# Two of four blocks of a four-tap filter, from VectorE products to diagonal matmuls on TensorE

## The chip, the cores and the metric

The kernel runs on one core of a Trainium2 chip. The metric is the device time of one execution in microseconds (us). The profile names the engines PE (TensorE, with its weight loads PEld), DVE (VectorE), ACT (ScalarE), POOL (GpSimd) and SP (SyncE, which here only issues DMAs).

## The reference

Two independent parts share one kernel; their outputs lie side by side, 576 columns each, for 2048 rows.

```python
# A: sliding dilated attention, 32 heads of 18, 8 positions with a distance of 2
qkv = x @ wqkv
logits = einsum("bhsd,bhswd->bhsw", q, kg) * scale      # kg, vg: k, v at s - 2 w
o = einsum("bhsw,bhswd->bhsd", softmax(logits), vg)
a = o @ wo
# B: a long convolution over the sequence, per channel
for t in range(4):                                        # the four taps
    k_shift = k_shift + k_pad[:, t:t + S, :] * shift_k[:, 3 - t]
kv = k_shift * v
y = irfft(rfft(kv, 2 S) * rfft(ssm_k, 2 S))[:S] + kv * ssm_D
b = q * y
```

The change is in the four taps of B, k_shift, for rows 1024 to 2047.

## The kernel before

All data is bf16, all sums are made in PSUM in fp32. Part B cuts the 2048 rows into four blocks of 512. Each block of kv is transformed by matmuls with tables of sines (`x_unit`), so is each block of the filter (`filter_unit`), their products are made by DVE (`spectral_product`), summed by PE (`spectral_sum`), and turned back by PE (`inverse`). Part A projects q, k and v on PE (`project`), multiplies q and k on DVE (`pair_product`, L706), sums over a head on PE (`pair_sum`, L720), takes the softmax, multiplies by v on DVE (`weigh`, L813) and sums on PE (`weighted`, L824; `output`, L888).

There is no scheduler. Every step is a job with a short name, and the string ORDER at the top lists the jobs; they are written out in that order, and each engine does its own instructions in it, one after the other. The names that matter here:

- `Lk2`, `Lv2`, `Lk3`, `Lv3`: loads of blocks 2 and 3 of k and v, on SP (L184, L203). Blocks 0 and 1 are loaded ahead of the written order.
- `T0` to `T3`: the taps of a block (L511). k was loaded as seven shifted rows for each group of four, with the channel along the row, so that a tap is a product with `skb`, the taps spread over all partitions (L517), a sum (L520), and at the end a product with v (L536), all on DVE. The result, kv, lies in `xw` at `kv_of(i)`.
- `M30` and the like: `mirror` (L538), matmuls with the matrix `fold` on PE, which make sums and differences of a row and its mirror row. Rows from both halves of a block lie on even and odd partitions.
- `k00a`, `k00b`, `q13a` and the like: halves of a projection, four matmuls each (L322, 128 x 128 weights, 512 columns); the second half also has the last 64 channels as two matmuls of 64 rows (L333). `X5` transposes the last 64 channels of x.
- `L001`, `G001`: pair product on DVE and pair sum on PE. `K310`: filter unit. `F3`: folding of a filter block (L602), `Lf3` its transposing load (L213), `Lo3` and `Fr` small copies on POOL and SP. `x001`: transform of a block of kv. `Lw`, `RG0`: weights of v and their regrouping. `SV` opens the memory that the taps used for part A's products.
- `I0`, `I1`: tables for the way back (L397): matmuls with 128 x 64 weights and 128 columns, in pairs on the two column halves of the array.

PSUM is four buffers that are handed out in turn (`banks`); a step that asks for one waits until whoever had it has been copied out.

Of the kernel before, what the change touches and what calls it, by code (L numbers as in the profile page):

```python
# [19 lines left out]
ORDER = """  # L20
    T0 k03a' T1 S1 k03b I1 k02a k02b Lk2 Lv2 I0 k00a' Lk3 Lv3 M01 X5 k00b q10a Ex q10b Lf3 T2 Lo3 q13a' q13b
    k10a k10b T3 k13a' Lf2 k13b q12a q12b N2 Lo2 k01a M10 k01b Lf1 M00 k11a k11b q11a M11 q11b Lf0 N3 Lw SV L001
    k12a M20 k12b x001 M21 x021 q24a x020 q24b x000 Lo1 k24a Fr Lo0 Z2 N1 RG3 k24b RG2 F3 RG0 F2 L000 K310 G000
    K311 K210 K211 L002 K313 G001 RG4 F1 G002 L003 G003 K302 L004 G004 K301 L010 K212 L011 K303 K213 K203 N0 F0
    L012 K200 K300 G010 L013 K201 K312 K202 RG1 G011 G012 K113 K103 G013 L014 G014 K112 K102 K101 L100 K100 K010
    K111 K110 sm0a K001 K013 sm0b v24a' L101 v24b L102 G100 L103 G101 K012 sm0c sm0d U3 U2 K000 K011 K003 G102
    K002 D0 D1 v11a v11b G103 L104 G104 ak00 M30 v12a' v12b ak02 v01a ak01 L110 G110 M31 L111 G111 v01b v00a'
    L112 G112 L113 Wl v00b G113 x031 U1 L114 G114 V04 v10a' v10b A04 sm1a sm1b v02a v02b v03a' sm1c v03b x201
    V10 V11 sm1d V12 A10 v13a' v13b D2 x330 x310 x301 V13 A11 V20 V21 x200 x331 x230 x010 x221 A20 x321 V22 x210
    x011 V23 D3 V34 ax02 x220 x030 x300 D4 A21 V40 V41 A34 D5 O000' x211 V42 x320 x231 x111 x131 Tx2 A40 V43  # L30
    x120 x101 ax00 x130 ax01 V50 x121 x311 O001 A41 V51 O100' p000 x100 x110 O010 A50 V52 z000 O011' V53 O101
    A51 Tk2 p010 z010 ax10 O020' O021 p020 z020 O110' ak10 i000 p200 i02880 Q0 p100 z100 p101 p110 p111 Q1 z101
    i02881 i001 p121 p120 O111 z110 p201 z111 z120 p210 z121 O120 p211 z200 z210 z211 p212 z212 z201 p202 z202
    Tx3 p220 Tk3 p221 O030' p222 O121 b0288 z220 p301 z221 O031' p302 b00 z222 p303 i200 i100 g0 Q2 p300 y300
    p312 i12880 i201 i101 i12881 z300 z301 z303 p310 p311 y310 O130 b10 b1288 p313 g1 Q3 p322 O131' z310 p320
    z311 p321 z313 i22880 i300 b20 y320 p323 i22881 i301 b2288 g2 z320 z321 z323 b30 i3384L g30 g3384
"""
# [14 lines left out]
def kernel(  # L52
# [122 lines left out]
    def kTok(m):  # L175
        return view(Ks, k_at(m, 2), [[D, 4], [1, D]])
    kjs, vts = [], []

# [5 lines left out]
    def load_k(i):  # L184

        eng = nc.sync
        kj = sp1.tile([128, 7, D], BF16, name="kj", bufs=2)
# [13 lines left out]
        kjs.append(kj)  # L201

    def load_v(i):  # L203
        vt = sp1.tile([128, 4, D], BF16, name="vt", bufs=2)
        nc.sync.dma_start(vt[0:128:2], vf[BL * i:BL * i + 256, :].rearrange("(p c) d -> p c d", c=4))
        nc.sync.dma_start(vt[1:128:2], bass.AP(tensor=vf.tensor, offset=vf.offset + (BL * i + 256 + 3) * D,
                                              ap=[[4 * D, 64], [-D, 4], [1, D]]))
        vts.append(vt)

# [51 lines left out]
    for h in range(2):  # L261
# [6 lines left out]
    nc.gpsimd.tensor_scalar(flip2[:], flip[:], 2.0, None, op0=ALU.mult)  # L268
# [242 lines left out]
    def taps(i):  # L511
# [24 lines left out]
        tt(kv, kv, vt, ALU.mult)  # L536

    def mirror(i, n):  # L538

        kv = kv_of(i)  # L540
        pss, held = zip(*[banks("ps_fold") for _ in range(2)])
        for pm in range(2):
            for h in range(2):
                for e in range(2):
                    nc.tensor.matmul(pss[pm][64 * e:64 * e + 64, h, 0:HD], fold[:, 64 * pm:64 * pm + 64],  # L545
                                     kv[:, 2 * n + e, HD * h:HD * h + HD], start=True, stop=True, tile_position=(0, 64 * e))
        for pm in range(2):
            nc.scalar.activation(halves(kv[:, 2 * n + pm, :]), pss[pm][:, :, 0:HD], ACT.Copy)
        slots.extend(held)

    for i in range(NBL):
        job(f"T{i}", taps, i)
        for n in range(2):
# [582 lines left out]
```

## Time and profile before

| | |
|---|---|
| time, three runs | 206.07, 206.62, 206.96 us; median 206.62 |
| span of the profiled execution | 204.6 us |
| PE busy | 196.9 us, 2074 matmuls and 2074 weight loads |
| DVE busy | 192.3 us, 146 instructions |
| ACT busy | 155.6 us, 223 instructions |
| POOL busy | 60.8 us, 106 instructions |
| mean granted TensorE clock | 0.994 |

The span is what the profile shows of one execution, from the first to the last instruction. Its own time as a run is not listed apart; the median of the runs is 2.0 us above the span. In a group's row stand the line, the engine, the operation, out<-in, the shape and the count; then busy time and the mean of one in ns; then the idle time of the engine before it and what ended it. Matmuls are pipelined: the mean of one holds its way through the array, so the distance from one start to the next is read from the chain or the timeline. In a row of the chain or the timeline stand the start, the length, the engine, the line and the count. In a row of DMA issues the last number is the median time from issue to landing.

### The profile page before, as it was taken

The numbers are of one execution on the slowest core, as the hardware profiler recorded it, in microseconds if no ns is written. First come the engines' busy times: TensorE is split into PE (matmuls) and PEld (weight loads), VectorE is DVE, ScalarE is ACT, GpSimd is POOL, SyncE is SP. The second block draws the span as 40 slices with busy tenths as digits, with TensorE's granted clock in tenths as the row PEclk, the third lists the DMA queues.
The fourth block names the chain that finished last, engine by engine and source line by source line (L and its number), as shares of the span: only waits on it lengthen the run. The fifth ranks groups of instructions, "written<-read, shape, count | busy, mean of one in ns | idle before, by whom it ended". The sixth has DMA issues, their size and how long they took to land.

```text
span 204.6 us, 5004 instructions
## 1 busy us (share of the span) xinstructions
PE 196.9 (96%) x2074; PEld 109.9 (54%) x2074; DVE 192.3 (94%) x146; ACT 155.6 (76%) x223; POOL 60.8 (30%) x106
## 2 busy tenths in 40 slices
PE   7999999999989999999999999999999999999990
PEld 2543544334455646543245556776666767766660
DVE  7559999999999999999999999999999999899992
ACT  4788995678899999966578678886778767767760
POOL 8989500011348581400380000004090001030300
PEclk9999999999999999999999999999999999999997
DMA  6999899989509869999899990879989303944555
GB/s 197 280 293 306 175 289 373 214 177 281 169 3 146 111 82 185 167 180 222 157 235 216 248 244 34 141 183 334 186 227 233 100 28 122 227 130 145 153 182 150
DMA packets 34916, 38.48 MB, mean 188 GB/s; under 512 B 17523, under 2 KB 28911, under 8 KB 34894
## 3 DMA queue, kind: packets, MB, share of 16 engines
q1 hardware_dynamic: 26668, 24.29, 46.5%
q0 software_dynamic: 5760, 11.36, 29.5%
q10 hardware_dynamic: 2466, 2.51, 3.6%
q8 instruction: 16, 0.26, 0.5%
q14 instruction: 6, 0.05, 0.1%
HBM read 13.11 MB, written 4.72 MB: 87 GB/s over the span
## 4 chain that ended last, share of the span: by engine, by line
PE 88%; DMA 3%; ACT 2%; DVE 2%; issue 1%; SPq 1%; DVEq 0%
PE ps_proj L322 18%; PE ps_fx L682 8%; PE ps_wo L888 8%; PE ps_z L975 8%; PE ps_inv L1010 7%; PE ps_acc L824 7%; PE ps_fk L567 5%; PE ps_log L720 5%; DMA Ks<-in_A_x_dram 3%; PE ps_proj L333 3%; PE ps_proj L326 3%; PE ps_proj L439 3%; PE ps_fk L568 3%; PE ps_fold L545 2%; PE ps_wo L880 1%
## 5 line engine op out<-in xcount | busy, mean ns | idle before, releaser
L322 PE MATMUL ps_proj<-xw 128*128 128x512 bf16 x160 | 38.5, 380 | 0.0
L706 DVE TENSOR_TENSOR av<-qk 128x4096 bf16<-128x4096 bf16 (+1 forms) x16 | 31.7, 2014 | 0.1
L322 PEld LDWEIGHTS <-xw 128*128 128x128 bf16 x160 | 13.9, 98 | 19.4 <-issue 5.7
L988 ACT ACTIVATE av<-ps_z 128x768 bf16<-128x768 f32 x23 | 17.2, 811 | 6.5 <-PE ps_z L975 6.0
L517 DVE TENSOR_TENSOR tB<-kj,skb 128x4608 bf16<-128x4608 bf16 (+1 forms) x8 | 19.3, 2416 | 0.1
L950 DVE TENSOR_TENSOR qk<-xw,Ks 128x2304 bf16<-128x2304 bf16 x14 | 18.9, 1354 | 0.3 <-PE ps_z L975 0.3
L684 ACT ACTIVATE xw<-ps_fx 128x576 bf16<-128x576 f32 x32 | 18.6, 665 | 0.3 <-PE ps_fx L682 0.2
L618 ACT ACTIVATE Ks<-ps_fk 128x576 bf16<-128x576 f32 x32 | 18.6, 699 | 0.2 <-PE ps_fk L568 0.2
L355 ACT ACTIVATE qk<-ps_proj 128x1024 bf16<-128x1024 f32 x14 | 14.3, 1023 | 5.2 <-PE ps_proj L333 2.8
L888 PE MATMUL ps_wo<-qk 128*128 128x288 bf16 x128 | 17.9, 287 | 0.0
L626 POOL DMA_DIRECT2D Ks<-Ks x8 | 10.1, 1426 | 26.0 <-PE ps_back L1059 19.3
L682 PE MATMUL ps_fx<-xw,TB 128*128 128x288 bf16 x128 | 17.7, 287 | 0.0
L567 PE MATMUL ps_fk<-Ks,TB 128*128 128x384 bf16 x62 | 16.5, 327 | 0.1
L824 PE MATMUL ps_acc<-av,ident 64*64 64x512 bf16 x160 | 15.3, 378 | 0.0
L1010 PE MATMUL ps_inv<-av,TI 128*128 128x288 bf16 (+1 forms) x112 | 15.2, 292 | 0.0
L568 PE MATMUL ps_fk<-Ks,TB 128*128 128x192 bf16 x62 | 15.2, 246 | 0.0
L682 PEld LDWEIGHTS <-TB 128*128 128x128 bf16 x128 | 11.9, 98 | 5.9 <-issue 2.7
L888 PEld LDWEIGHTS <-qk 128*128 128x128 bf16 x128 | 11.7, 98 | 5.4 <-issue 2.7
L355 ACT ACTIVATE v<-ps_proj 128x1024 bf16<-128x1024 f32 x9 | 9.3, 1033 | 6.5 <-PE ps_proj L322 4.5
L813 DVE TENSOR_TENSOR av<-Ks,v 128x4096 bf16<-128x4096 bf16 x6 | 13.5, 2286 | 0.0
L827 ACT ACTIVATE qk<-ps_acc 128x1024 bf16<-128x1024 f32 x8 | 8.2, 1024 | 6.7 <-PE ps_acc L824 6.7
L1010 PEld LDWEIGHTS <-TI 128*128 128x128 bf16 x112 | 10.6, 98 | 4.2 <-issue 1.1
(195 smaller groups left out, 441.6 us busy)
## 6 DMA issues: line engine op xcount, KB each, us to landing
Ks<-Ks POOLq DMA_DIRECT2D x8, 576.0 KB, 7.8
TB<-av SPq DMA_DIRECT2D x12, 256.0 KB, 5.4
kj<-in_B_k_dram SPq DMA_DIRECT2D x6, 504.0 KB, 7.0
vt<-in_B_v_dram SPq DMA_DIRECT2D x8, 288.0 KB, 5.3
Ks<-av SPq DMA_DIRECT2D x8, 256.0 KB, 5.6
out_dram<-qk ACTq DMA_DIRECT2D x5, 288.0 KB, 3.7
Ks<-in_A_x_dram SPq DMA_DIRECT2D x2, 576.0 KB, 5.4
xw<-in_A_wqkv_dram SPq DMA_DIRECT2D x2, 576.0 KB, 6.2
```

The costliest lines, as they stand in the source:

```text
L322: nc.tensor.matmul(ps[:, jp, :], wq(kb, comp, 128 * ct, 128), xT(kb, 1024 * jj + 512 * jp, 512), **se)
L355: nc.scalar.activation(view(t, o + pad + 1024 * jj, [[512, 2], [1, 512]]), ps[:], ACT.Copy)
L517: tt(to, view(kj, row * D, [[D, n], [D, 4], [1, D]]), view(skb, row * D, [[D, n], [0, 4], [1, D]]), ALU.mult)
L567: nc.tensor.matmul(o[:, 0:2], w, rhs[:, 0:2], start=start, stop=stop)
L568: nc.tensor.matmul(o[:, 2], w, rhs[:, 2], start=start, stop=stop)
L618: nc.scalar.activation(view(Ks, k_at(m, cs ^ (m & 1)) + 96 * gi, [[768, 3], [384, 2], [1, 96]]), acc3(ps), ACT.Copy, scale=(PSG, MSG)[cs][ ...
L682: nc.tensor.matmul(ps[:, pm, 0:HD], TX[:, 2 * pm + c, 128 * gi:128 * gi + 128], kv[:, 2 * c + pm, HD * h:HD * h + HD], start=(c == 0), sto ...
L706: tt(view(P, at, [[step, 4], [256, nj], [1, 256]]), view(t, o + 256 * hh, [[0, 4], [512, nj], [1, 256]]), view(tk, ok + 2 + 8 * ug + 256 * ...
L824: nc.tensor.matmul(acc[64 * o:64 * o + 64, h, :], ident[64 * h:64 * h + 64, 64 * h:64 * h + 64], view(P[s], 256 * u, [[2048, 2], [1, 256]] ...
L888: nc.tensor.matmul(ps[:, r, 0:HD], oT(hh, j + 2 * r, t)[:, o:o + 128], wo[:, t // 2, t % 2, HD * h:HD * h + HD], start=(t == 0 and not fli ...
L950: tt(product_home(n), view(xw, HB * XG[i] + QTR * t, [[HB, 3], [1, QTR]]), view(Ks, k_at(j - i, 0) + QTR * t, [[HB, 3], [1, QTR]]), ALU.mult)
L1010: nc.tensor.matmul(ps[:, c, 0:n], TI[:, sl, pm, 128 * c:128 * c + 128], Yall(j % 2, pm, sl, slice(c0, c0 + n)), start=(pm == 0 and sl == 0 ...
```

## The change

`T2` and `T3` are replaced by `T20 T21 T2t` and `T30 T31 T3t`. For these two blocks k is loaded transposed, with the channel on the partition, by two DMA transposes (528 x 512, and 528 x 128 for the last 64 channels), and v goes straight to its place in `xw`, first half of the block on partitions 0 to 63, second half on 64 to 127. A tap is then a matmul whose weights are 64 rows of the transposed k, every fourth column from an offset, and whose moving operand is a 128 x 128 diagonal of that tap's 128 weights; four taps add up in PSUM. A half of a block (`T20`) is 64 such matmuls, in pairs on the two column halves; the tail (`T2t`) is 32 with 64 x 64 weights and 64 columns. DVE multiplies the sum in PSUM by v. The diagonals are made once on POOL (`Wd`) from the identity and from the taps, which two loads on ACT's queue bring in. Block 2's transposed k and the diagonals lie in free parts of `Ks`, block 3's in the buffer of block 0's k. As the halves now lie on the partitions otherwise, the mirrors of blocks 2 and 3 use a second matrix, `fold_t`, also made on POOL. The ORDER string is new throughout; the jobs other than these, and all code ahead of the written order but the loads and POOL's two products for `fold_t`, are the same.

```diff
-    T0 k03a' T1 S1 k03b I1 k02a k02b Lk2 Lv2 I0 k00a' Lk3 Lv3 M01 X5 k00b q10a Ex q10b Lf3 T2 Lo3 q13a' q13b
+    k00a' S1 k02a k03a' k00b T0 k01a k01b T1 Wd k02b X5 k12a k11a k03b q12a q12b k12b Ex k10a k10b Lk3 Lv3 T30
+    q10a Lw RG2 RG3 T31 T3t SV Lf0 L002 q10b RG0 q11a q11b k11b L000 M00 Lf2 N2 Lf3 k13a' RG4 q13a' q13b k13b
...
+    taps_w = main.tile([128, 5, 4], BF16, name="taps_w")
+    nc.scalar.dma_start(taps_w[:, 0:4, :], B_shift_k[0:512, :].rearrange("(kb p) j -> p kb j", p=128))
+    nc.scalar.dma_start(taps_w[64:128, 4, :], B_shift_k[512:576, :])
...
+    TURNED = (2, 3)
+    KT = 16 + BL
+    diag = view(Ks, 3 * HB, [[512, 4], [128, 4], [1, 128]])
+    diag_t = view(Ks, 3 * HB + 2048, [[64, 4], [1, 64]])[64:128]
...
+        if i in TURNED:
+            t = view(Ks, 0, [[1, 5 * KT]]) if i == TURNED[0] else sp1.tile([128, 7, D], BF16, name="kj", bufs=2)
+            rows = kf[BL * i - 16:BL * i + BL]
+            eng.dma_start_transpose(view(t, 0, [[KT, 4], [1, KT]]), rows[:, 0:512])
+            eng.dma_start_transpose(view(t, 4 * KT, [[1, KT]]), rows[:, 448:576])
...
+    fold_t = main.tile([128, 128], BF16, name="fold_t")
+    for h in range(2):
+        nc.gpsimd.tensor_tensor(fold_t[:, 64 * h:64 * h + 64], ident[:, 0:64], flip[:, 0:64], (ALU.add, ALU.subtract)[h])
...
+    def tap_diagonals():
+        nc.gpsimd.tensor_tensor(diag, ident[:].unsqueeze(1).unsqueeze(1).to_broadcast([128, 4, 4, 128]),
+                                taps_w[:, 0:4, :].unsqueeze(3).to_broadcast([128, 4, 4, 128]), ALU.mult)
+        nc.gpsimd.tensor_tensor(diag_t, ident[64:128, 64:128].unsqueeze(1).to_broadcast([64, 4, 64]),
+                                taps_w[64:128, 4, :].unsqueeze(2).to_broadcast([64, 4, 64]), ALU.mult)
+
+    def turned(i, kb, c, j, e):
+        return view(kjs[i], KT * kb + 16 + (259 - c if e else c) - j, [[4, 64]])
+
+    def taps_pe(i, h):
+        ps, slot = banks("ps_tap")
+        for c in range(2):
+            for kb in range(4):
+                for j in (3, 2, 1, 0):
+                    for e in range(2):
+                        nc.tensor.matmul(ps[64 * e:64 * e + 64, c, 128 * kb:128 * kb + 128],
+                                         turned(i, kb, 2 * h + c, j, e), diag[:, kb, j, :],
+                                         start=(j == 3), stop=(j == 0), tile_position=(0, 64 * e))
+        kv = kv_of(i)[:, 2 * h:2 * h + 2, 0:512]
+        tt(kv, ps[:], kv, ALU.mult)
+        slots.append(slot)
+
+    def taps_pe_tail(i):
+        ps, slot = banks("ps_tap")
+        for c in range(4):
+            for j in (3, 2, 1, 0):
+                for e in range(2):
+                    nc.tensor.matmul(ps[64 * e:64 * e + 64, 0, 64 * c:64 * c + 64], turned(i, 4, c, j, e)[64:128],
+                                     diag_t[:, j, :], start=(j == 3), stop=(j == 0), tile_position=(64, 64 * e))
+        kv = kv_of(i)[:, :, 512:576]
+        tt(kv, view(ps, 0, [[64, 4], [1, 64]]), kv, ALU.mult)
+        slots.append(slot)
```

Line numbers after the change are larger: L517 became L540, L520 L543, L536 L559, L590 L652, L706 L768; the new lines are L562 and L564 (diagonals), L576 (taps), L580 (their product with v), L588 and L591 (the tail's).

On DVE, the place where the taps end and the pair products of part A (L706, out of qk) begin. Before, the end of T2, all of T3, then a small negation of a filter row (L590), then pair products:

```order
L536 TENSOR_TENSOR xw<-xw,vt 128x2304
L517 TENSOR_TENSOR tB<-kj,skb 128x4608
L520 TENSOR_TENSOR xw<-tB 128x2304
L517 TENSOR_TENSOR tB<-kj,skb 128x4608
L520 TENSOR_TENSOR xw<-xw,tB 128x2304 x2
L536 TENSOR_TENSOR xw<-xw,vt 128x2304
L590 TENSOR_SCALAR Ks<-Ks 1x576 x2
L706 TENSOR_TENSOR av<-qk 128x4096
```

After, from the end of T1: the three products with v for block 3 out of PSUM (ps_tap), then pair products at once.

```order
L543 TENSOR_TENSOR xw<-xw,tB 128x2304 x2
L559 TENSOR_TENSOR xw<-xw,vt 128x2304
L580 TENSOR_TENSOR xw<-ps_tap,xw 128x2x512 x2
L591 TENSOR_TENSOR xw<-ps_tap,xw 128x4x64
L768 TENSOR_TENSOR v<-qk 128x4x1024
L768 TENSOR_TENSOR av<-qk 128x4096
L652 TENSOR_SCALAR Ks<-Ks 1x576
```

T2's and T3's twelve instructions are gone from ahead of the pair products; block 2's products with v come later, between pair products.

On POOL, the place behind the set-up work. Before, the small writes into the table TB (L504) are followed by copies of filter rows inside Ks (L650) and by the load of ssm_D (L579):

```order
L367 MEMSET qk 128x4x16
L369 MEMSET qk 64x16
L502 MEMSET TB 1x512
L504 MEMSET TB 1x128 x4
L650 DMA Ks<-Ks 128x576 x3
L579 DMA Ks<-in_B_ssm_D_dram 1x16x36
```

After, the two products that make the diagonals stand between them, and the copy of a piece of k (L381, before L358) comes ahead of the filter rows:

```order
L525 MEMSET TB 1x512
L527 MEMSET TB 1x128 x4
L562 TENSOR_TENSOR Ks<-ident,taps_w 128x2048
L564 TENSOR_TENSOR Ks<-ident,taps_w 64x256
L381 DMA qk<-qk 64x16
L641 DMA Ks<-in_B_ssm_D_dram 1x16x36
```

So the diagonals are the first thing that POOL does after its set-up, and all its DMAs of the filter stage stand behind them.

On PE, the first tap matmuls, those of block 3, between halves of projections (L345 and L356 are L322 and L333 of before); kj is the transposed k as weights, Ks holds the diagonals:

```order
L345 MATMUL ps_proj<-xw 128x512
L356 LDWEIGHTS xw
L356 MATMUL ps_proj<-xw 128x512
L576 LDWEIGHTS kj
L576 MATMUL ps_tap<-Ks,kj 64x128
```

Before, PE had no instruction of the taps; 256 of L576 and 64 of L588 are added to its stream.

More of the change, by code (lines that the diff above doesn't have):

```diff
@@ L26 @@
[L26 to L35, printed above, removed]
@@ L37 @@
+    O030' i200 b1288 i22880 i101 i201 O031' p300 y300 z300 p312 p310 y310 z301 i22881 z303 b10 p311 p313 O130
+    O021 z310 z311 z313 p322 O131' g1 i300 p320 p321 y320 O120 O121 p323 b20 b2288 g2 i301 z320 z321 z323 b30 Q3
+    i3384L g30 g3384
 """
@@ L186, in load_k @@
         eng = nc.sync
+        if i in TURNED:
[3 more added lines that the diff above has]
+            eng.dma_start_transpose(view(t, 4 * KT, [[1, KT]]), rows[:, 448:576])
+            kjs[i] = t
+            return
         kj = sp1.tile([128, 7, D], BF16, name="kj", bufs=2)
@@ L544, in mirror @@
                 for e in range(2):
-                    nc.tensor.matmul(pss[pm][64 * e:64 * e + 64, h, 0:HD], fold[:, 64 * pm:64 * pm + 64],
+                    nc.tensor.matmul(pss[pm][64 * e:64 * e + 64, h, 0:HD], (fold_t if i in TURNED else fold)[:, 64 * pm:64 * pm + 64],
                                      kv[:, 2 * n + e, HD * h:HD * h + HD], start=True, stop=True, tile_position=(0, 64 * e))
@@ L549, in mirror @@
         slots.extend(held)
+    job("Wd", tap_diagonals)
     for i in range(NBL):
-        job(f"T{i}", taps, i)
+        if i in TURNED:
+            for h in range(2):
+                job(f"T{i}{h}", taps_pe, i, h)
+            job(f"T{i}t", taps_pe_tail, i)
+        else:
+            job(f"T{i}", taps, i)
         for n in range(2):
```

28 lines of the change are left out of this document (20 added, 8 removed).

## The prediction

> **What bounds the kernel now.** I read the page first, for the share of each engine and for the chain that ended last.
>
> ```profile
> span 204.6 us, 5004 instructions
> PE 196.9 (96%) x2074; PEld 109.9 (54%) x2074; DVE 192.3 (94%) x146; ACT 155.6 (76%) x223; POOL 60.8 (30%) x106
> PE 88%; DMA 3%; ACT 2%; DVE 2%; issue 1%; SPq 1%; DVEq 0%
> ```
>
> Two engines are nearly full, TensorE (96%) and VectorE (94%), so the change takes from one full engine and gives to the other. The chain runs through PE for 88% of the span. A busy PE may still hide waiting, so the next views ask whether it does. The first is the table of busy time by stretches of 20 us (columns: PE, its weight loads, DVE, ACT, POOL, the granted clock, DMA).
>
> ```profile
> 40.00:60.00 20.00, 19.65 (x146) 9.26 (x144) 19.61 (x15) 17.09 (x23) 4.32 (x9) 1.00 0.74 174
> 60.00:80.00 20.00, 19.59 (x191) 11.43 (x192) 19.86 (x16) 19.95 (x34) 14.10 (x14) 1.00 0.81 116
> 140.00:160.00 20.00, 20.00 (x267) 13.68 (x264) 19.96 (x15) 15.94 (x23) 7.12 (x9) 1.00 0.97 226
> ```
>
> No stretch leaves PE or DVE more than half a microsecond, and the clock is granted in full. The second view is PE's own waits, without the two before its first projection:
>
> ```profile
> PE ps_log L720 <- DVE av L706: 0.6, 1, 0.6
> PE ps_inv L1029 <- ACT av L988: 0.3, 1, 0.3
> PE ps_back L1038 <- ACT v L1031: 0.2, 1, 0.2
> PE ps_z L975 <- DVE Ks L950: 0.2, 1, 0.2
> ```
>
> They sum to 1.3 us, of which DVE causes 0.8. The third is the chain in order of time, where runs of equal matmuls give PE's own pace:
>
> ```profile
> 20.42 0.57 PE ps_ti L397 x16
> 20.99 1.83 PE ps_proj L322 x8
> 22.82 0.32 PE ps_proj L333 x2
> ...
> 25.62 0.25 PE ps_x L428 x8
> ...
> 29.10 3.56 PE ps_proj L322 x16
> ...
> 68.62 0.16 PE ps_fk L567
> 68.87 0.16 PE ps_fk L567
> ...
> 104.71 1.00 PE ps_acc L838 x32
> ```
>
> Sixteen projection matmuls of 512 columns take 3.56 us and eight take 1.83: 0.216 us for each further one, and 0.10 us left over for each run. That 0.10 us I read as the price of changing the way the array is divided (128x128 to 64-row halves and back). In the filter stage a pair of 384 and 192 columns starts every 0.25 us (68.62 to 68.87); 576 columns at 0.216 per 512 are 0.243. So PE goes at its own pace even there, where ACT is fullest (19.95 of 20). PE is the bound from about 10 us to the end, with at most 1.3 us to give back; DVE is a second engine that just keeps up.
>
> **The change part by part.** *What DVE loses and gains.* The rows with shapes kept apart:
>
> ```profile
> L517 DVE TENSOR_TENSOR tB<-kj,skb 128x4608 bf16<-128x4608 bf16 x7 | 17.9, 2556 | 0.1
> L536 DVE TENSOR_TENSOR xw<-xw,vt 128x2304 bf16<-128x2304 bf16 x4 | 5.4, 1358 | 0.1
> L520 DVE TENSOR_TENSOR xw<-tB 128x2304 bf16<-128x2304 bf16 x3 | 4.1, 1358 | 0.1
> L1020 DVE TENSOR_TENSOR TB<-ps_back,TB 128x384 bf16<-128x384 f32 x2 | 1.0, 554 | 0.6 <-PE ps_back L1038 0.6
> L1020 DVE TENSOR_TENSOR TB<-ps_back,TB 128x768 bf16<-128x768 f32 x1 | 1.0, 954 | 0.0
> ```
>
> Each of T2 and T3 is two products of 2.556, three sums of 1.358 and one product with v of 1.358: 10.5 us, 21.1 us for both. In come four products out of PSUM of 1024 elements and two of 256. The L1020 rows give (954 - 554)/384 = 1.04 ns for each element, so about 1.22 and 0.42 us: 5.7 us. DVE loses 15.4 us net. Off the bound that is worth only the waits that PE has for DVE, 0.8 us.
>
> *What PE gains.* 256 matmuls with 128 x 64 weights and 128 columns, in pairs on the two column halves. The nearest row is L397, the same shape in the same pairs: (0.57 - 0.10)/16 = 0.029 us each, 7.4 us in all (6.9 at the pace of the columns alone, 64 of 512 at 0.216 us; 9.1 with the 0.57 undivided). 64 tail matmuls, 64 x 64 weights and 64 columns: not in the trace; between 0.9 us (columns alone at the pace above, two at a time) and 2.3 (0.0356 each, the L397 run undivided). I take L838, the nearest row of that array shape: (1.00 - 0.10)/32 = 0.028, 1.8 us. PE's stream, read from the order with each line's array shape, changes shape 133 times before and 159 times after; 26 x 0.10 = 2.6 us (3.4 at 0.13). Mirrors with the other folding matrix cost what they did. PE has no idle stretch to hide any of this, so all of it counts: 7.4 + 1.8 + 2.6 = 11.8 us.
>
> The Trainium skill, "TensorE: Matmul & The Clock Gate", section "Back-to-back issue gap", states about 81 ns for each matmul of 128 columns in a stream of weight loads and matmuls. By it the 256 would take 20.7 us, and the sum would be 13.3 us larger. The trace speaks against it: L397 keeps 29 ns over 16.
>
> *The new wait on PE at T30.* T30 needs the diagonals (two products on POOL), the transposed k of block 3, and everything behind it on PE waits with it. The rows, of the chain, the timeline, the groups and the DMA issues:
>
> ```profile
> 18.38 0.22 PE ps_proj L333
> 22.71 0.63 POOL L504 MEMSET TB<- 1x128 bf16 x4
> 24.97 0.66 SPq L206 DMA_DIRECT2D vt<-in_B_v_dram  x1
> 32.45 1.36 DVE L536 TENSOR_TENSOR xw<-xw,vt 128x2304 bf16<-128x2304 bf16 x1
> L268 POOL TENSOR_SCALAR flip<-flip 128x128 bf16<-128x128 bf16 x1 | 0.5, 524 | 0.0
> L298 POOL TENSOR_SCALAR ident<-ident 128x128 bf16<-128x128 bf16 x1 | 1.5, 1513 | 0.0
> xw<-in_A_x_dram SPq DMA_TRANSPOSE x2, 6.8
> 43.35 0.63 POOL L650 DMA_DIRECT2D Ks<-Ks  x1 [20.01 <-DVE xw L520]
> L545 PEld LDWEIGHTS <-fold 128*64 128x64 bf16 x64 | 2.9, 109 | 3.2 <-issue 2.6 <-DVE xw L520 0.4
> ```
>
> PE starts the written order at 18.38 (first row). Ahead of T30 stand 14 half projections of four matmuls (14 x 4 x 0.216 = 12.1), six tails (0.32 with their change of shape, 1.9), X5 (0.25) and some nine more changes (0.9): PE is there at 33.5. POOL is free at 23.3 (22.71 + 0.63) and was then idle for 20 us, which hides the two small folding products and the start of the diagonals. The large product has 16 times the elements of a 128 x 128 operation. That took 0.524 us when DVE was quiet (L268) and 1.513 beside DVE's products (L298). All quiet, it ends at 23.3 + 0.7 + 8.4 = 32.4, ahead of PE. At DVE's side until T1 ends at 33.8 (32.45 + 1.36), then quiet, it has done 9.8/1.513 = 6.5 parts and needs 9.5 x 0.524 = 5.0 more: 38.8, and PE waits 5.3. SP issues Lk3 at 25.6 (after L206), and a transpose lands in 6.8: 32.4, in time, by about a microsecond. I take 1.0 us of wait here, near the quiet end, because DVE runs out of work at 33.8; 0 to 5.3 stay for the range. For T2 the loads stand on SP behind those of wv and four filter transposes; PE comes to T21 only behind the first folded filter, which needs three of the same four, so I cost it at nothing, and if the two loads are late there too, it is a case of C.
>
> *Costed at nothing:* the two loads of the taps on ACT's queue (cover: ACT's waits for PE's first results; uncovered, two issues of 0.66 like L206's), the K and V loads removed, and the copies behind the diagonals on POOL, which wait for ACT and for filters that come later.
>
> Sum: 11.8 - 0.8 + 1.0 = 12.0 us. The profiled span was 204.6, so 216.6 for its like; the median of the three runs is 206.62, 2.0 us more than that span for what lies around it, so 206.6 + 12.0 = 218.6 us.
>
> **The rivals.**
>
> *A, DVE was the bound (faster).* For it: DVE is 94% busy, and PE's busy time is modelled. If PE only followed DVE, 15.4 us of DVE's work less would give 206.6 - 15.4 = 191.2 at best. It decides only if PE's 196.9 us hold more than the 11.8 us of added work as hidden waiting; with 15 us hidden the time would be about 203. Against it: the pace of 0.216 us and the 0.25 us pairs. Chance 0.04.
>
> *B, no net change.* The order hides the taps in the waits and saves changes of shape elsewhere. The waits are 1.3 us and the changes go up, not down. It would give 205.6 to 207.7. Chance 0.03.
>
> *C, T30 starves PE.* Diagonals or transposes come late, by the slow pace of POOL above: 5.3 instead of 1.0, 222.9; up to 13 late if DVE's gaps are not used at all (16 x 1.513 from 24.0 is 48.2, 229). For: the L298 row; against: DVE has nothing to do after T1 but wait for T30. Chance 0.17.
> The other way round, POOL's product could hold up T1's last products by its 8.4 us: T1 ends at 42.2, T30's PSUM buffer comes free at 43.4, and PE, back at that buffer after T31, T3t and q10 (about 5 to 7 us after 33.5, at 40.7), waits 2.7: 220.3. Chance 0.06. The Trainium skill, "SBUF — State Buffer", section "Who interferes with whom", says that a VectorE instruction with two SBUF inputs and a GpSimd one that reads SBUF exclude each other, and that the first to issue has the port for its whole length. The rows agree in one direction (L298 against L268); no row shows DVE held up.
>
> *D, the weight loads set the pace.* The taps' weights are read with a step of four elements, which no row has. If each load of 0.109 us (the L545 row) were no longer hidden, two halves at a time, a tap matmul would cost 0.055 instead of 0.029: 320 x 0.026 = 8.3 us more, 226.9. Chance 0.08.
>
> **How the numbers follow.** The forecast has 0.62; A 0.04, B 0.03, C 0.23 in its two forms, D 0.08. The forecast's bounds: 6.9 + 0.9 + 2.6 - 1.3 = 9.1 at the low end, 215.7; 7.4 + 2.3 + 3.4 + 2.5 = 15.6, 222.2 at the high end. The range reaches on to C's main value and a little past it, and a microsecond under the low end: 214.5 to 224.5; outside lie A, B, D and the far end of C, with about 0.18. A measurement of this kernel can tell about 0.5% from no change, 1.0 us. Faster 0.05, within 0.5% 0.03, slower 0.92.
>
> **What would show it.** In the profile after: PE busy near 210 us of a span near 216, DVE near 177 with idle time whose releaser is PE; the tap runs of 64 matmuls at about 1.9 us each; PE waiting at most a microsecond before the first tap matmul, for POOL. A wait of 5 us there is C; tap runs of 3.5 us are D. PE's run of projections still at 0.216 us but the span at or under 206 would make the prediction wrong: then the 133 changes and the waits that I called small held more than I read from them.

## The result, and the profile after

| | time, us | ratio to before, 95% interval |
|---|---|---|
| before | 206.36 median of 6 runs, 206.07 to 206.96 | |
| after | 228.53 median of 6 runs, 228.00 to 231.15 | 1.1096, 1.1043 to 1.1149 |
| forecast | 218.6, range 214.5 to 224.5 | |

The change makes the kernel 22.2 us slower. The direction was forecast, and the size was not: the result lies 9.9 us above the forecast and 4.0 above its range. The profiled execution took 229.66 us and has a span of 227.7, 23.1 more than the span before. First the page of after, as the page of before was read:

```profile
span 227.7 us, 5622 instructions
PE 210.9 (93%) x2382; PEld 120.2 (53%) x2394; DVE 182.2 (80%) x140; ACT 156.9 (69%) x223; POOL 73.3 (32%) x110
PE   7999999999999969999951999999999999999991
PEclk9999999999999999999997699999999999999997
...
PE 84%; DMA 5%; DVE 4%; ACT 2%; SPq 2%; issue 1%; DVEq 0%; ACTq 0%
```

PE's busy time is near the forecast 210, but the span is 12 us above the forecast 216. DVE fell by 10.1 us only (the forecast was 15.4) and has idle time now; 3.6 of the missing 5.3 us are two sums of T1 that took longer beside POOL (shown below). In the row of PE's 40 slices, of 5.7 us each, a hole (5 and 1) stands between 114 and 125 us, and the granted clock is low behind it. PE's waits name it:

```profile
PE ps_acc L900 <- DVE av L875: 7.2, 1, 7.2
PE ps_log L782 <- ACT v L378: 1.7, 1, 1.7
...
PE ps_proj L345 <- issue: 1.1, 6, 0.3
```

The last row is no wait: the trace has records of 149 of the 160 matmuls of L345, and the gaps of about 0.16 us stand where one is missing, at a full clock too. L900 sums the tail of part A's first chunk after its softmax (job `A04`; L838 of before), L875 makes its products with v (`V04`, L813 of before). DVE does not come late because it is busy. Its timeline (start, length, and in brackets the idle time ahead with what ended it), then PE's:

```profile
111.66 2.29 DVE L875 TENSOR_TENSOR av<-Ks,v 128x4096 bf16<-128x4096 bf16 x1 [0.72 <-PE ps_acc L886]
121.95 2.29 DVE L875 TENSOR_TENSOR av<-TB,v 128x4096 bf16<-128x4096 bf16 x1 [8.00 <-DMA TB<-av]
```

```profile
124.30 1.92 PE L900 MATMUL ps_acc<-av,ident 64*64 64x256 bf16 x32 [7.17 <-DVE av L875]
```

DVE waits 8.0 us for TB, into which four DMAs on SP's queue (`D0`, 256 KB each) spread the weights of the softmax over the partitions. Two answers on DMAs give SP's issues with the median time from issue to landing; the first is before, 86 to 100 us, the second is after, 100 to 123 us.

```profile
TB<-av SPq DMA_DIRECT2D x4, 256.0 KB, 5.3
Ks<-av SPq DMA_DIRECT2D x4, 256.0 KB, 5.8
```

```profile
TB<-av SPq DMA_DIRECT2D x4, 256.0 KB, 12.3
qk<-av SPq DMA_DIRECT2D x4, 256.0 KB, 10.4
```

The first row of each is `D0`: the same four transfers take 12.3 us instead of 5.3. What runs beside them stands in POOL's timelines: first before, where `D0` was issued at 89 and had landed by 97, then after, where it was issued from 106.2 on.

```profile
85.34 1.19 POOL L626 DMA_DIRECT2D Ks<-Ks  x1 [2.22 <-DMA Ks<-Ks]
100.57 1.26 POOL L862 DMA_DIRECT2D qk<-in_A_wo_dram  x2 [14.04 <-DVE av L706]
...
104.02 2.54 POOL L626 DMA_DIRECT2D Ks<-Ks  x2
```

```profile
98.91 2.48 POOL L688 DMA_DIRECT2D Ks<-Ks  x2 [16.63 <-ACT Ks L680]
101.04 1.61 POOL L924 DMA_DIRECT2D qk<-in_A_wo_dram  x2
...
106.43 1.24 POOL L688 DMA_DIRECT2D Ks<-Ks  x1 [1.53 <-ACT av L786]
```

Before, the load of wo (`Wl`, six DMAs) was held for 14.04 us by a pair product of DVE, and so came 11.6 us after `D0`. Of the filter sums (copies that add to their destination, two of 576 KB each), `U3` and `U2` were issued ahead of `D0`, the last one at 85.34, and `U1` behind `Wl`. `D0` writes into TB, which the filter units read. SP's waits of after name these units (L630) for its spreads (L856):

```profile
SPq L856 <- PE ps_fk L630: 13.7, 3, 7.0
```

So `D0` must wait for the last filter unit; its last matmul starts at 105.8 in after and started at 88.3 before. Next come the last pair products on DVE and the issue of `D0` on SP, each before and then after:

```profile
91.32 10.08 DVE L706 TENSOR_TENSOR av<-qk 128x4096 bf16<-128x4096 bf16 x5
96.24 5.63 DVE L768 TENSOR_TENSOR av<-qk 128x4096 bf16<-128x4096 bf16 x3 [1.42 <-PE ps_log L782]
```

```profile
89.01 3.15 SPq L794 DMA_DIRECT2D TB<-av  x4
106.16 5.98 SPq L856 DMA_DIRECT2D TB<-av  x4
```

The pair products end at nearly the same time, 101.4 before and 101.9 after. It is `D0` that has moved, by 17 us: the old ORDER writes it ahead of the last pair products (`L110` to `L114`), the new one behind all of them and behind filter units that follow them. So `Wl`, which came 11.6 us after `D0`, is now issued 5.1 us ahead of it, with `U3` just before and `U2` just behind (106.43 and 110.45). The table by stretches of after shows the queue that this makes (the last three columns are clock, DMA share and GB/s):

```profile
80.00:100.00 20.00, 18.13 (x164) 8.62 (x158) 15.46 (x9) 14.91 (x23) 3.33 (x7) 1.00 0.34 55
100.00:120.00 20.00, 16.76 (x133) 8.12 (x134) 11.67 (x10) 14.41 (x20) 7.33 (x10) 1.00 1.06 220
120.00:140.00 20.00, 15.21 (x159) 7.95 (x162) 14.74 (x9) 9.51 (x14) 2.38 (x2) 0.83 1.03 217
```

The DMA engines are two thirds idle from 80 to 100 us and full for the 40 us behind. The share alone does not make a spread slow: before has 0.97 from 80 to 100 us, where `D0` took 5.3. What differs is how much POOL's queue moves beside it (q0 in the two DMA answers): 0.79 MB in the 14 us before, 3.03 MB in the 23 us after. Last, the taps themselves on PE's timeline:

```profile
34.81 2.21 PE L576 MATMUL ps_tap<-Ks,kj 128*64 128x128 bf16 x64
36.96 1.04 PE L345 MATMUL ps_proj<-xw 128*128 128x512 bf16 x3
37.92 2.21 PE L576 MATMUL ps_tap<-Ks,kj 128*64 128x128 bf16 x64
```

PE comes to `T30` at 34.81 and waits for nothing there. A half takes 36.96 - 34.81 = 2.15 us with its change of shape; the forecast was about 1.9 without it.

### The profile page after: what moved, and what is told of

The parts are those of the page before. It is cut to its first block, busy times and chain, and to the rows that moved or that the text cites. A ratio compares the mean times of both kernels' runs of the same rounds, so it can differ in the third digit from the quotient of the medians.

```text
span 227.7 us, 5622 instructions
## 1 busy us (share of the span) xinstructions
PE 210.9 (93%) x2382; PEld 120.2 (53%) x2394; DVE 182.2 (80%) x140; ACT 156.9 (69%) x223; POOL 73.3 (32%) x110
## 4 chain that ended last, share of the span: by engine, by line
PE 84%; DMA 5%; DVE 4%; ACT 2%; SPq 2%; issue 1%; DVEq 0%; ACTq 0%
PE ps_proj L345 12%; PE ps_z L1037 8%; PE ps_wo L950 7%; PE ps_fx L744 7%; PE ps_inv L1072 7%; PE ps_acc L886 6%; DMA TB<-av 5%; PE ps_log L782 4%; PE ps_fk L629 4%; PE ps_tap L576 4%; PE ps_proj L462 3%; PE ps_proj L349 2%; PE ps_proj L356 2%; PE ps_rev L664 2%; PE ps_fold L601 2%; PE ps_fk L630 2%
## 5 line engine op out<-in xcount | busy, mean ns | idle before, releaser
L768 DVE TENSOR_TENSOR av<-qk 128x4096 bf16<-128x4096 bf16 (+1 forms) x16 | 32.0, 2021 | 8.9 <-PE ps_log L782 5.2
L345 PE MATMUL ps_proj<-xw 128*128 128x512 bf16 x149 | 37.5, 384 | 1.4 <-issue 1.1
L345 PEld LDWEIGHTS <-xw 128*128 128x128 bf16 x160 | 14.1, 98 | 18.4 <-issue 5.0
L680 ACT ACTIVATE Ks<-ps_fk 128x576 bf16<-128x576 f32 x32 | 19.2, 652 | 5.4 <-PE ps_fk L630 5.1
L1072 PE MATMUL ps_inv<-av,TI 128*128 128x288 bf16 (+1 forms) x112 | 16.1, 293 | 0.0
L875 DVE TENSOR_TENSOR av<-TB,v 128x4096 bf16<-128x4096 bf16 x4 | 9.1, 2285 | 8.0 <-DMA TB<-av 8.0
L886 PE MATMUL ps_acc<-av,ident 64*64 64x512 bf16 x160 | 15.3, 379 | 0.0
L630 PE MATMUL ps_fk<-Ks,TB 128*128 128x192 bf16 x62 | 15.2, 246 | 0.0
L875 DVE TENSOR_TENSOR av<-Ks,v 128x4096 bf16<-128x4096 bf16 x6 | 13.6, 2289 | 1.4 <-PE ps_acc L886 1.0
L688 POOL DMA_DIRECT2D xw<-xw x2 | 2.4, 1214 | 32.7 <-ACT qk L889 32.7
```

Of the source, the lines that this page charges most:

```text
L345: nc.tensor.matmul(ps[:, jp, :], wq(kb, comp, 128 * ct, 128), xT(kb, 1024 * jj + 512 * jp, 512), **se)
L630: nc.tensor.matmul(o[:, 2], w, rhs[:, 2], start=start, stop=stop)
L680: nc.scalar.activation(view(Ks, k_at(m, cs ^ (m & 1)) + 96 * gi, [[768, 3], [384, 2], [1, 96]]), acc3(ps), ACT.Copy, scale=(PSG, MSG)[cs][ ...
L768: tt(view(P, at, [[step, 4], [256, nj], [1, 256]]), view(t, o + 256 * hh, [[0, 4], [512, nj], [1, 256]]), view(tk, ok + 2 + 8 * ug + 256 * ...
L875: tt(view(weight_home(n, ct), 0, [[2048, 2], [256, W], [1, 256]]), view(t, at, [[step, 2], [256, W], [1, 256]]), view(late["v"], voff + 2 ...
L886: nc.tensor.matmul(acc[64 * o:64 * o + 64, h, :], ident[64 * h:64 * h + 64, 64 * h:64 * h + 64], view(P[s], 256 * u, [[2048, 2], [1, 256]] ...
```

## The experiments

The theory after the result: about 12 us of the 22 are PE's own added work, as forecast, and the rest is the pile-up of transfers that the new order makes around `D0`. The rivals: the taps and the changes of shape cost PE more than thought; or the low clock behind the wait costs it.

Times are given as microseconds over the kernel before on the same chip: the ratio less 1, times the 206.2 to 206.95 us of before. After is 22.6 by that measure. An interval of 0.005 to either side is 1.0 us; those of e5 and e8 rest on two executions each.

| run | what it is | ratio, 95% interval | over before |
|---|---|---|---|
| e1_gate | after; Wl, U2, U1 behind A04 | 1.0873, 1.0819 to 1.0926 | 18.0 |
| e2_old_order | taps on PE, order of before | 1.0679, 1.0632 to 1.0725 | 14.0 |
| e3_fill | after; dummy work ahead of A04 | 1.1093, 1.1073 to 1.1112 | 22.5 |
| e4_gate_u2 | after; U2, U1 behind A04 | 1.1191, 1.1162 to 1.1220 | 24.6 |
| e5_filters_first | after; filters of blocks 3, 2 first | 1.1164, 1.1069 to 1.1259 | 24.0 |
| e6_one_tap | e2, one tap of four | 1.0453, 1.0382 to 1.0525 | 9.3 |
| e7_one_block | e2, block 3 alone on PE | 1.0618, 1.0576 to 1.0659 | 12.7 |
| e8_first_gate | e5; Wl, U1 behind A04 | 1.0952, 1.0886 to 1.1018 | 19.6 |
| e9_one_block_late | e7, T3 group later | 1.0304, 1.0260 to 1.0348 | 6.3 |
| e10_one_tap_late | e6, T3 group later | 1.0253, 1.0186 to 1.0319 | 5.2 |
| e11_all_late | e2, T3 group later | 1.0610, 1.0576 to 1.0643 | 12.6 |
| e12_shapes | before, 66 more changes of shape | 1.0429, 1.0402 to 1.0456 | 8.9 |
| e13_no_loads | after without Wl, U2, U1 | 1.0658, 1.0590 to 1.0725 | 13.6 |
| e14_old_no_loads | e2 without Wl, U2, U1 | 1.0543, 1.0520 to 1.0566 | 11.2 |

### Holding the transfers back: e1, e4

In e1 a job `PG` ahead of `Wl` makes POOL copy one element of what A04 brings out, so that `Wl` and all behind it on POOL come after it.

```diff
-    x231 A20 V22 x320 x031 x230 Wl x301
+    x231 A20 V22 x320 x031 x230 PG Wl x301
+    scr = main.tile([1, 8], BF16, name="scr")
+    job("PG", lambda: nc.gpsimd.tensor_copy(scr[0:1, 0:1], view(qk, 4096, [[1, 1]])[0:1]))
```

> POOL waits, by a copy of one element of the result of A04, before the load of wo and the sums U2 and U1, so that they can't share the DMA engines with D0, the spread of the softmax weights that V04 needs. Pile-up theory: D0 lands in 5 to 7 us after its issue instead of 9 to 12, PE's wait of 7.2 us at A04's first matmul (L900) falls to under 2, the clock stays at 0.99 or more, 217 to 220 us. Rival (D0 is issued too late, behind the last filter unit; the DMAs beside it do not matter): the wait stays at 5 us or more, 226 to 229. Rival (POOL's sums are themselves needed early): the wait at L900 goes and one of the same size comes behind it at the first spectral products.

Measured: 18.0 us over before, 4.6 less than after, but above the 217 to 220 expected. The DMA answer for the same stretch, and PE's longest wait:

```profile
TB<-av SPq DMA_DIRECT2D x8, 256.0 KB, 5.0
```

```profile
PE ps_acc L886 <- DVE av L875: 3.9, 1, 3.9
```

The transfers into TB, eight in this stretch, land in 5.0 us again and the wait ahead of A04 is gone. But a new one of 3.9 us stands 26 us later (at 143 us): `Wl` and `U2` now run beside a later spread, `D4`. The pile-up has moved, not gone.

In e4 the same `PG` stands ahead of `U2`; `Wl` stays early.

> As the first of this set, but only U2 and U1 wait for A04's result; the load of wo stays early. If the sums of U2 (two of 576 KB, read, added and written) are what delays D0: as good as the first, 217 to 220 us. If wo's six loads (0.8 MB) do it: the wait at L900 stays at 4 to 7 us, 222 to 228.

Measured: 24.6 us, no gain (more than after, and above what was expected). `Wl`, with `U3`, is enough to slow `D0`; `U3` alone is not, for it stands ahead of `D0` in e1 too:

```profile
TB<-av SPq DMA_DIRECT2D x4, 256.0 KB, 10.4
```

```profile
PE ps_acc L900 <- DVE av L875: 5.0, 1, 5.0
PE ps_acc L886 <- DVE av L875: 4.0, 2, 2.0
```

### The taps in the order of before: e2

```diff
-    k00a' S1 k02a k03a' k00b T0 k01a k01b T1 Wd k02b X5 k12a k11a k03b q12a q12b k12b Ex k10a k10b Lk3 Lv3 T30
+    T0 k03a' T1 S1 Wd k03b I1 k02a k02b Lk2 Lv2 I0 k00a' Lk3 Lv3 M01 X5 k00b q10a Ex q10b Lf3 Lo3 q13a' q13b
+    k10a k10b T20 k13a' Lf2 k13b T21 q12a q12b T2t N2 Lo2 k01a M10 k01b T30 Lf1 M00 k11a k11b T31 q11a M11 q11b T3t Lf0
```

The rest of ORDER is that of before.

> The taps on PE, but the written order of before; only the jobs of T2 and T3 are replaced, one tap job behind each of some later projection halves, and the diagonals made behind S1. Theory (the added PE work is about 12 us, the rest came from the new order's pile-up): 217 to 220 us, no wait of PE above 2 us, clock 0.99. Rival (the taps themselves cost PE 20 us or more): 226 or more.

Measured: 14.0 us over before. So 8.6 of the 22.6 us come from the order, not from the taps. PE's waits have nothing left of the spreads:

```profile
PE ps_fk L628 <- DMA Ks<-Ks: 0.9, 1, 0.9
PE ps_fk L628 <- ACT Ks L666: 0.7, 1, 0.7
PE ps_tap L575 <- POOL Ks L561: 0.3, 1, 0.3
```

DVE has lost the work of T2 and T3 here as in after, and still POOL waits for it, longer than before (14.04). SP's issue of `D0`, then POOL's of `Wl`:

```profile
101.76 3.33 SPq L855 DMA_DIRECT2D TB<-av  x4
```

```profile
113.59 1.26 POOL L923 DMA_DIRECT2D qk<-in_A_wo_dram  x2 [14.71 <-DVE av L767]
```

`Wl` comes 11.8 us after `D0`, as before the change (11.6), and `D0` lands in 4.8 us. So it is the new written order, and not the work that DVE lost, that brings the two together.

### Is it the low clock: e3

28 dummy matmuls of 512 columns fill PE's wait ahead of A04.

```diff
-    v11b A04
+    v11b FL A04
+        for _ in range(28):
+            nc.tensor.matmul(ps[:, 0, :], ident[:], view(TB, XO, [[1, 512]]), start=True, stop=True)
```

> The changed kernel with 28 matmuls of 512 columns, whose result nobody reads, ahead of A04, where PE waits 7.2 us. At 0.216 us they take 6.0, less than the wait. If the clock drop behind the wait costs time of its own (0.83 granted from 120 to 140 us, about 3.4 us): the clock stays at 0.99, and the time falls by 2 to 4 us, to 224.5 to 226.5. If the drop costs nothing: 228 to 229.

Measured: 22.5 us over before, as after. The clock is back, as the stretch that had 0.83 shows:

```profile
120.00:140.00 20.00, 18.79 (x193) 9.75 (x195) 16.29 (x10) 11.15 (x17) 2.38 (x2) 1.00 1.02 218
```

It brought nothing. What PE gains in pace it waits elsewhere: 1.2 us are left ahead of A04, and 1.4 stand ahead of L886, where after waits for nothing. The spreads set the time there and not PE. The rival of the clock falls.

### Moving the filters instead: e5, e8

If the late filter units were the cause, because `D0` waits for them, then the filter sums should be brought forward. e5 writes the units of blocks 3 and 2 first and `U2` right behind `U3`; e8 adds the `PG` of e1.

```diff
-    sm1b U3 A10
+    sm1b U3 U2 A10
```

> The changed kernel's written order, with one thing mended: in the 32 places of the filter units the units stand so that all of filter blocks 3 and 2 come first, then block 1, then block 0 (the order of before), and U2 stands right behind U3. POOL's sums U3 and U2 then start some 5 us earlier and should be through, or nearly, when D0 is issued. If the new order's late filter units are what piled the DMAs up: D0 lands in 4 to 7 us, PE's wait at A04 is under 2 us and no wait of 4 us takes its place, 218 to 222 us. If the pile-up has another cause (part A's products standing earlier, wo's load): 224 to 229.

Measured: 24.0 us; PE waits 7.9 us ahead of A04, no less than before the move. `U2`, `Wl` and `U1` now all run beside `D0`, whose transfers take 11.0 us. `D0` itself is issued at 107.4, no earlier than in after, for the last filter unit stands where it stood. So this run does not show what an earlier `D0` would bring.

> The last two filter groups of k first (as in e5), and also the load of wo and the filter load that follows it made to wait for the result of A04. If the cost of the new order is that D0's four transfers share the DMA engines with that load and the filter sums, D0 lands in under 6 us, the wait of TensorE ahead of A04 is under 2 us and the time is 219 to 222 us, near the 220.1 of the old order. If the order costs something else (work of TensorE or VectorE itself), the transfers land early but the time stays at 224 us (e1) or above. If the moved filter load (U1) now holds up a later spread, a wait of 3 us or more appears there instead and the time is 223 to 226.

Measured: 19.6 us, by its interval no better than e1. The four transfers into Ks behind it take 10.1 us, with `Wl` and `U1` beside them, and PE waits 1.9 and 2.0 us for spreads. That is the third case of the expectation, with smaller waits. In each of the four places tried within this order (e1, e4, e5 and e8) these transfers meet a spread.

### Leaving the transfers out: e13, e14

`Wl`, `U2` and `U1` are left out altogether, in the order of after (e13) and in the order of before (e14); what they would bring is missing in the output, and all else is as it was.

```diff
-            job(f"U{m}", turn_filter, m)
+            if m == 3: job(f"U{m}", turn_filter, m)
-    job("Wl", load_wo)
```

> The changed kernel with the load of wo and the filter sums U2 and U1 left out altogether (the output is then another one: what they would have brought is missing). The order of all else stays. If their transfers beside D0 and D4 are what the new order costs, D0 lands in 4 to 6 us, TensorE's waits ahead of A04 and ahead of the later sums are under 1 us each, and the time is 220 to 223 us: 5 to 8 under the changed kernel, and over the old order without the same loads (e14) only by 19 further changes of shape (2.3 us) and the 1.7 us wait for ScalarE. If the order costs TensorE or VectorE something else, it stays at 225 to 228.

> The old order (e2) with the load of wo and U2 and U1 left out in the same way: the base for e13. In e2 the spreads land in 4 to 5 us and TensorE waits for none of them, so by the same theory this is within a microsecond of e2's 220.1 (219 to 220.5). If these transfers slow other things in any order, it is 216 to 218.

Measured: 13.6 and 11.2 us over before. In the new order the three transfers cost 22.6 - 13.6 = 9.0 us, in the old one 14.0 - 11.2 = 2.8, where about none was expected. The gap between the orders falls from 8.6 to 2.4 us, with about 1.5 us to either side by the intervals; 4.0 was expected, from further changes of shape and the wait ahead of L782. In e13 the spread lands in 5.0 us, and DVE's product follows without idle time (the same two rows as shown of after):

```profile
TB<-av SPq DMA_DIRECT2D x8, 256.0 KB, 5.0
```

```profile
110.94 2.29 DVE L875 TENSOR_TENSOR av<-Ks,v 128x4096 bf16<-128x4096 bf16 x1 [0.67 <-PE ps_acc L886]
113.15 2.29 DVE L875 TENSOR_TENSOR av<-TB,v 128x4096 bf16<-128x4096 bf16 x1
```

The wait ahead of A04 is not among PE's waits any more, and `D0` is issued at 105.4, as late as in after. So it is the company of the transfers that costs, not their start. POOL's queue moves 1.18 MB in the 23 us here, and 3.03 in after.

### What the taps cost PE: e6, e7, e9, e10, e11

e6 makes only one of the four taps (the other three are left out of the result); e7 turns only block 3. Both keep the order of e2.

```diff
-                for j in (3, 2, 1, 0):
+                for j in (0,):
```

```diff
-    TURNED = (2, 3)
+    TURNED = (3,)
```

> The taps on PE in the order of before, with one of the four taps only: the other three are left out, so that PE has 192 + 48 fewer matmuls and everything else (loads, diagonals, products with v, changes of shape) stays. If PE is the bound throughout and a tap matmul costs 0.030 to 0.032 us: 7 to 7.7 us less than with four taps, 212.5 to 213.5. If part of the tap matmuls lay beside other waits: less than 4 us gained, 216 or more.

> The order of before with block 3's taps on PE and block 2's on DVE as they were. If PE is the bound and DVE's relief is worth nothing beyond its 0.8 us of waits: half of the price of two blocks, 212 to 214.5. If DVE was a bound too and relief of one block already serves: 207 or less.

Measured: 9.3 and 12.7 us, and e7 fits neither case of its expectation. Three quarters of the taps saved 4.7 us of e2's 14.0, one block of two 1.3 only. The waits tell why, here of e7, with the rows of DVE and POOL that lie behind them:

```profile
PE ps_tap L575 <- DVE xw L579: 3.7, 1, 3.7
```

```profile
31.55 4.94 DVE L558 TENSOR_TENSOR xw<-xw,vt 128x2304 bf16<-128x2304 bf16 x1
```

```profile
31.68 3.60 POOL L561 TENSOR_TENSOR Ks<-ident,taps_w 128x2048 bf16<-128x2048 bf16 x1
```

DVE's last product of T1, which takes 1.36 us elsewhere, takes 4.94: POOL's large product began 0.13 us after it and ended at 35.28, and DVE's at 36.49. In e7 DVE then still has T2 to do, so the products with v out of PSUM come late and PE finds the buffer taken. In e9 and e10 the three entries of T3 stand together, later:

```diff
-    k01b T30 Lf1 M00 k11a k11b T31 q11a M11 q11b T3t Lf0
+    k01b Lf1 M00 k11a k11b q11a M11 q11b T30 T31 T3t Lf0
```

> Only block 3 by diagonals (as in e7), with the three entries T30, T31 and T3t put together ahead of Lf0, so that TensorE no longer waits for the buffers that VectorE's work on T1 holds. If e7's 219.2 came from that 3.7 us wait and the low clock behind it, the wait goes and the time is 212.5 to 214.5 us (half of the diagonals' work on TensorE, 206.2 plus 6 to 8). If the wait was hidden anyway, the time stays at 218 to 219.5.

> One of the four taps only (three left out, as in e6), with T30, T31 and T3t together ahead of Lf0. If TensorE's own work sets the time and e6 lost part of its gain in a wait of 2.5 us for VectorE's buffers, the time is 212 to 214 us, 6 to 8 under the old order with all four taps (220.1). If what the taps add on TensorE is not what sets the time, it stays at 215.5 to 217.

Measured: 6.3 and 5.2 us, so half of e7's 12.7 us went when the entries were moved; what the 3.7 us wait alone was worth is not shown apart. e9 gives PE's pace over 128 matmuls in one row:

```profile
45.28 4.18 PE L575 MATMUL ps_tap<-Ks 128*64 128x128 bf16 x128
49.39 1.18 PE L587 MATMUL ps_tap<-Ks 64*64 64x64 bf16 x32
```

From 45.28 to 49.39 are 4.11 us, less a change of shape 4.0: 0.031 us for each.

e11 has all four taps of both blocks in this place.

> All four taps of both blocks on TensorE, in the order of before as in e2, with T30, T31 and T3t together ahead of Lf0. If TensorE's own work sets the time, two blocks cost twice the 6.8 us of the one block of e9: 219 to 220 us, and the three further taps against e10 (192 + 48 matmuls) cost 7.5 to 8.5 us. If what separates e2 from e10 is mostly e2's waits ahead of T30, the time is 216 to 218.

Measured: 12.6 us, twice the 6.3 of one block. Against e10 it has 192 + 48 more matmuls and no other change: 12.6 - 5.2 = 7.4 us, 0.031 us each, with about 1.5 us to either side of the 7.4 by the two intervals; e9's row has the same pace. The whole of the 320 is then 9.9 us.

### What a change of shape costs: e12

The kernel before, with a dummy of 64 x 64 weights and 64 columns behind the first three matmuls of 11 half projections.

```diff
+                    if jp == 0 and not first and kb < 3:
+                        nc.tensor.matmul(ps[0:64, 1, 0:64], wq(0, comp, 0, 64)[0:64], xT(0, 0, 64)[0:64],
+                                         start=True, stop=True, tile_position=(0, 0))
```

> The kernel before, with 33 dummy matmuls of 64 x 64 weights and 64 columns put between 128 x 128 projection matmuls (into a part of PSUM that is overwritten later): 66 more changes of the array's shape, nothing else. If a change costs 0.10 us, as the prediction read it, the time is 206.2 + 6.6 + 33 x 0.03 = 213.8 us (212.5 to 215). If most of the 0.10 us left over in a run is the run's own fill and not the change, it is 207 to 210.

Measured: 8.9 us. Less 33 x 0.03 for the dummies, 7.9 us for 66 changes: 0.12 each. The timeline shows it singly:

```profile
32.90 0.39 PE L322 MATMUL ps_proj<-xw 128*128 128x512 bf16 x1
33.22 0.21 PE L324 MATMUL ps_proj<-xw 64*64 64x64 bf16 x1
33.37 0.39 PE L322 MATMUL ps_proj<-xw 128*128 128x512 bf16 x1
```

From one full matmul to the next are 0.47 us instead of 0.216. The dummy and two changes take 0.25, so a change takes (0.25 - 0.03)/2 = 0.11.

## Why the prediction was wrong

The account by its own steps, in us, with the spans of the two profiled executions:

| step | predicted | measured |
|---|---|---|
| taps and tails on PE | 9.2 | 9.9 (320 x 0.031, e11 against e10) |
| 26 more changes of shape | 2.6 | 3.0 (26 x 0.115, e12) |
| PE's waits for DVE that go | -0.8 | -0.6 (the one ahead of the pair sums; 0.2 stays) |
| the wait at T30 | 1.0 | 0 |
| other new waits of PE | 0 | 8.9 (7.2 ahead of A04, 1.7 ahead of L782) |
| PE's work at the low clock behind the wait | 0 | 2.2 |
| sum | 12.0 | 23.4, of 23.1 in the spans |

The 2.2 us are read from the same jobs in after and in e13, from the first matmul of A04 to the second run of L345 behind it: 130.04 - 124.30 = 5.74 us (the row of 124.30 is shown above) and 119.85 - 116.33 = 3.52.

```profile
130.04 1.04 PE L345 MATMUL ps_proj<-xw 128*128 128x512 bf16 x4
```

```profile
116.33 1.07 PE L900 MATMUL ps_acc<-av,ident 64*64 64x256 bf16 x32
119.85 1.04 PE L345 MATMUL ps_proj<-xw 128*128 128x512 bf16 x4
```

They lie on PE's path in after, but e3 shows that the kernel is no faster without them.

**The step that failed** is "Costed at nothing": "the copies behind the diagonals on POOL, which wait for ACT and for filters that come later". The prediction followed PE's stream and the taps' own loads. It took the order to be new only around the taps and looked for a wait at `T30` and `T2` alone, so its sum has no term for the rest of the new order. But ORDER was new throughout, and POOL's queue holds more than copies: the load of wo and three filter sums of twice 576 KB. The order alone costs 8.6 us (22.6 of after less the 14.0 of e2, which has the same taps in the old order). It writes the last filter units, and `D0` with them, behind the last pair products, so that `D0` shares the DMA engines with `Wl` and `U2`. Before, only the last copy of `U2` reached into it (issued at 85.34, landing in 6.3 us). DVE's relief is not what did it: in e2 POOL waits 14.71 us for DVE all the same. e1 (the spread lands in 5.0 us when the transfers are held) and e13 against e14 (without the transfers the gap between the orders falls from 8.6 to 2.4 us) show that the transfers are the cause of most of it. The forecast of 12.0 us fits the kernels without the pile-up within 2.0: 14.0 (e2), 12.6 (e11), 13.6 (e13), 11.2 (e14).

The Trainium skill, "DMA: Bandwidth & Descriptors", section "Issuing engines are not separate DMA queues", says that transfers started from SP, ACT and POOL run on the same 16 engines and interleave, whoever issued them. The rows agree: `D0` on SP's queue goes from 5.3 to 12.3 us beside POOL's transfers, with the DMA share at 1.06.

**Changes of shape and pace.** Both were read rightly from the rows of before, which is why the added work on PE came out. The 0.10 us left over per run was the change of shape indeed (0.11 to 0.12 when measured by itself), and a tap matmul takes 0.031 instead of 0.029. Together they are 1.1 us of the miss.

**The wait at T30 (rival C, first form).** It did not come. The large product took 3.59 us, not the 8.4 to 24 that 16 times a 128 x 128 operation gave. The rows were of another, smaller operation, and with 16 times its elements the product took 2.4 to 6.9 times its time (1.513 and 0.524 us). It also ran later than forecast, and ended at 30.64 + 3.59 = 34.23, just ahead of PE's 34.81; PE was 1.3 us later than worked out. The far end of C has a wrong sum besides: POOL's 48.2 is 14.7 us behind PE's 33.5, not 13, which gives 232.3 by the prediction's own terms and not 229. The 2.5 us of wait and the 0.13 us for a change of shape in the upper bound rest on no row that it shows; measured were 0 and 0.11 to 0.12. POOL's and DVE's rows of after:

```profile
30.64 3.59 POOL L562 TENSOR_TENSOR Ks<-ident,taps_w 128x2048 bf16<-128x2048 bf16 x1
```

```profile
29.12 6.32 DVE L543 TENSOR_TENSOR xw<-xw,tB 128x2304 bf16<-128x2304 bf16 x2
```

**The second form of C** was right in its mechanism. Two sums of 1.36 us each took 6.32, 3.6 us more, beside POOL's product. The Trainium skill, "SBUF — State Buffer", section "Who interferes with whom", has VectorE and GpSimd exclude each other at the shared port; the prediction said that no row shows DVE held up, and this one does, as does e7's 4.94. That the first to issue has the port for its whole length, as the prediction cites it, is not what the rows show by their starts: in e7 DVE's product began 0.13 us ahead of POOL's and still ended 1.21 us behind it. In after PE had other work and waited for nothing there. In e6 and e7 PE waits 2.5 and 3.7 us for DVE's products with v; how much of that is the hold-up is not shown.

**The other rivals.** A (DVE was the bound) would have made the kernel faster: DVE lost 10.1 us of work and the time rose, and 66 mere changes of shape on PE cost 8.9 us (e12), so PE was the bound with nothing hidden. D (the weight loads set the pace, 0.055 us) is refuted by 0.031 us over 128 matmuls in a row, although the taps' weight loads took longer than the 0.109 us of the row it used (a median of 0.147 in after, from kj). The Trainium skill's 81 ns of "TensorE: Matmul & The Clock Gate", section "Back-to-back issue gap", do not hold for these pairs either.

**What stays open.** The old order with the taps has between 11.2 and 14.0 us over before by run (e14, e11, e2), and its waits explain only a part of that scatter. Why e10, with a quarter of the taps, still costs 5.2 us is not fully accounted for: 80 x 0.031 and 7 x 0.115 us are 3.3, and e11 has the same 1.9 us more than its 320 matmuls and 7 changes. The 2.4 us that the new order still costs without the transfers were not taken apart. The 1.7 us wait ahead of L782 was not tried by itself; it stays in e1 and e13.

## What to carry to other kernels

When a change comes with a new written order, the order is a change of its own and needs its own line in the sum: run it apart from the work that moved, as e2 did. List in the trace of before which waits keep two bursts of transfers apart, above all on queues that are far from the change, and ask for each whether it still does so in the new order. For each transfer on which the bound engine depends, look at what else is in flight at its time, before and in the new order; holding the others back helps only if there is a place for them that meets no other such transfer (e1 gained 4.6 us and met a later spread; e4 and e5 gained nothing). And where an engine is the bound and never idle, price the work moved onto it by the nearest rows: here that part was right within 1.1 us of 11.8.

## What of the hardware was not expected

- Four transfers of 256 KB from one part of SBUF to another land in a median of 4.8 to 5.3 us where POOL's queue moves 0.79 MB in 14 us (before) or 1.18 to 1.40 MB in 23 us (e13, e1, e2), and in 10.4 to 12.3 where it moves 1.92 to 3.08 MB in 23 us (e4, after, e5). The DMA share does not tell the two apart: it is 0.97 in before and 1.06 in after around them. The adding copies themselves went from a median of 7.8 us before to 9.8 after.
- In the last part of an idle stretch of 7.2 us PE's granted clock fell, to 0.50 from 124 to 128 us (0.83 over the 20 us from 120), and then came back to 1.00. Filling the stretch with dummy matmuls kept it at 1.00, and the time stayed the same (22.5 and 22.6 us over before).
- A GpSimd product of 128 x 2048 elements took 3.59 us, although another operation on 128 x 128 took 0.524 to 1.513 us: the time per element is 2.3 to 6.7 times lower for the large one.
